# Two-stage routed attention and experts on one core: the second pair's preparation moved by two blocks, the output stage's rests on VectorE, value products copied by ScalarE, projections interleaved

## The chip, the cores and the metric

The kernel runs on one core of one Trainium2 chip. A core has TensorE (matrix products into PSUM), VectorE, ScalarE and GpSimd (elementwise work), and SyncE, which issues most of the transfers. Each engine works through its own list of instructions in the order in which they stand there; engines wait for each other through semaphores. The time is device microseconds of one execution, median of the runs shown; lower is better.

## What is computed

Three layers, one behind the other: attention with a cluster mask, a mixture of experts, and a gated convolution with an output projection.

```python
# attention, B=2, H=8, S=768, D=64
mask = q_assign[:, :, :, None] == k_assign[:, :, None, :]      # argmax over 16 centroids
attn = softmax(where(mask, q @ k.T / 8, -1e9));  out = attn @ v
# experts: every token goes to one of E=8, d_model 512, hidden 1024
h = np.maximum(x[b, s] @ w1[e], 0.0);  out[b, s] = p[e] * (h @ w2[e])
# last layer, per batch b: 768 tokens, 512 channels, 5 taps
gate = 1 / (1 + exp(-sum_k conv_w[k] * xp[:, k:k + S, :]))
return (gate * (x @ w_val)) @ w_out
```

## The kernel before

The program is written in one order by hand; every engine gets its instructions in that order, and each pool of buffers makes a writer wait until the buffer's last readers are done.

**Attention.** Eight pairs of heads, twelve blocks (`i`) to a pair; a block is one head and 128 queries against 768 keys. Block `i` issues the scores of block `i + 2` (`do_S`, L601: two products at L607 from the stacked tile `st`, two at L611 that also need its rows 64 to 79), transposes its own weights (`do_T`, L642), takes the exponential of block `i + 2` (`do_exp`) and at odd blocks a part of the product with V (L654). The next pair is prepared in six groups of steps (`prep_steps`, L322 and on), one group to a block, at `i % 12` = 0 to 5 (L769): keys rounded and centroid products (`k_hi`, `dots1`); queries (`q_hi`, `k_lo`, `dots2`); `argmax1` and `argmax2`; `q_lo` and six transfers `stack1` into `st`; `argmax3` and `argmax4`; `rows`, `rows_out` and four transfers `stack2`, which bring rows 64 to 79. Scores of the next pair are first wanted at `i % 12` = 10. Input tiles of keys and queries have one buffer, so the second pair's loads wait for the first pair's steps. All these transfers stand in SyncE's queue. The first pair's preparation stands in one list ahead of the loop, with five products without a use (`spin1`) between the first scores and the one-hot transposes (L438).

**Between attention and experts.** Tokens are scattered to expert slots by GpSimd's queue and read back by SyncE's (L897). TensorE meanwhile does 34 products without a use (`spin3`, bfloat16, 512 columns).

**Experts.** From L912 on TensorE transposes tokens and runs three products of rounded parts for every product (`hi` x `hi`, `hi` x rest, rest x `hi`), all in a 4-byte rounded type (fp32r) with 256 or 512 columns.

**Output stage** (L1054 to the end). Tokens are transposed (L1092), ScalarE rounds them (`xh`, L1096), a copy `xf` is kept, and GpSimd forms the rests `xl` = `xf` - `xh` (L1101). There are eight (batch, 128 channels) blocks. For each: the convolution is one ScalarE product and four VectorE multiply-adds (L1114), ScalarE takes the sigmoid (L1119), TensorE forms the value product in PSUM (L1128 to L1134, 24 products of 384 columns), VectorE multiplies both (L1147, which reads PSUM and so frees it), ScalarE rounds (`gh`, L1148) and GpSimd forms the rest `gl` (L1149). The projection of 128 tokens is twelve products of 512 columns (L1160 to L1163), copied out by ScalarE (L1164) and stored. In batch 1, `x2_tiles(1, ...)` stands ahead of the sigmoid, and six of the twelve projections stand behind the last block.

Of the kernel before, what the change touches and what calls it, by code (L numbers as in the profile page):

```python
# [18 lines left out]
S = 768  # L19
# [13 lines left out]
def routed_attention_moe_kernel(  # L33
# [45 lines left out]
    def load_kq(g, between=()):  # L79
# [3 lines left out]
        for dst, src in between:  # L83
            nc.sync.dma_start(dst, src)
        nc.sync.dma_start(X[g][:, 1, :], kq[b, p, :, 1, :])
# [8 lines left out]
    load_kq(0, [(cent_sb, cent), (cd, cdiag)])  # L94
# [11 lines left out]
    keep_warm(ps_m.tile([128, 512], F32, tag="m", name="spin0"), 9)  # L106

# [214 lines left out]
    def prep_steps(g):  # L322
# [413 lines left out]
    for grp in prep_steps(0):  # L736
        for f in grp:
            f()
    load_v(0)
    load_kq(1)  # L740
# [7 lines left out]
    for i in range(NI):  # L748
# [20 lines left out]
        if i % 12 < len(prep):  # L769
            for f in prep[i % 12]:  # L770
# [45 lines left out]
    keep_warm(ps_t.tile([128, 512], F32, tag="t", name="spin3"), 34)  # L816
# [261 lines left out]
    def x2_tiles(b, t0, n, eng):  # L1078
# [14 lines left out]
        for i in range(n):  # L1093
# [14 lines left out]
    def conv0(b, d):  # L1108
        G[b, d] = fl.tile([128, S], F32, tag="gt", name="gt", bufs=4)
# [11 lines left out]
    V = {}  # L1121
# [18 lines left out]

    def gated(b, d):
# [3 lines left out]
        gt, vp = G.pop((b, d)), V.pop((b, d))  # L1145
        gv = gt.rearrange("p (a c) -> p a c", a=2)
# [4 lines left out]
    def project(b, t, parts=1):  # L1151
        ts = slice(128 * t, 128 * t + 128)
        r0 = S * b + 128 * t
        os_ = fl.tile([128, 512], F32, tag="os", name="os")
        w = 512 // parts
        for n in range(parts):
            cs_ = slice(w * n, w * n + w)
            op = ps_x.tile([128, 512], F32, tag="x", name="op")
            for k in range(4):
                nc.tensor.matmul(op[:, :w], gh[b][:, k, ts], oh_[:, k, cs_], start=(k == 0), stop=False)  # L1160
                nc.tensor.matmul(op[:, :w], gh[b][:, k, ts], ol[:, k, cs_], start=False, stop=False)  # L1161
            for k in range(4):
                nc.tensor.matmul(op[:, :w], gl[b][:, k, ts], oh_[:, k, cs_], start=False, stop=(k == 3))  # L1163
            nc.scalar.copy(os_[:, cs_], op[:, :w])  # L1164
# [81 lines left out]
```

## Time and profile before

| | us |
|---|---|
| median of 3 runs | 584.48 (584.1 to 588.53) |
| the profiled execution, whole | 586.31 |
| its span, first to last instruction | 584.6 |
| TensorE busy | 553.5 (95%) |
| VectorE busy | 394.2 (67%) |
| ScalarE busy | 333.1 (57%) |
| GpSimd busy | 146.1 (25%) |

Attention takes the span's first 270 us, the experts stand from 282 to 484, the output stage from 489 to the end. A busy TensorE is not TensorE at its full clock: the page gives the granted clock apart. What one engine waits for is read from the timeline of a stretch, where each row has start, length, engine, line, operation, and in brackets the idle time ahead and what ended it.

### The profile page before, as it was taken

What the parts mean: (1) busy time and instruction counts of PE and PEld (TensorE: products, weight loads), DVE (VectorE), ACT (ScalarE), POOL (GpSimd) and SP (SyncE); (2) the same over time, 40 slices, a digit from 0 to 9 for tenths busy, and PEclk for the clock granted to TensorE, in tenths of its full rate; (3) what the DMA queues carried; (4) which work ended last, traced back from release to release, by engine and by line L of the source; (5) the groups of instructions that cost most, each with busy time, mean ns of one, the idle gap of its engine ahead of it and who ended that gap; (6) DMA issues with size and microseconds to landing.
All of it is one profiled execution on the core that took longest, in us unless ns stands there. A gap on an engine that the chain in (4) does not pass through costs nothing. (4 is left out here: it accounts for less than half of the span.)

```text
span 584.6 us, 9359 instructions
## 1 busy us (share of the span) xinstructions
PE 553.5 (95%) x3474; PEld 440.0 (75%) x3474; DVE 394.2 (67%) x644; ACT 333.1 (57%) x603; POOL 146.1 (25%) x121
## 2 busy tenths in 40 slices
PE   7799999999999999997899999999999996987997
PEld 3476767676767777774698988989989983885876
DVE  6376667676787876557378868769688361699940
ACT  3386868686868686852256545555564452453522
POOL 4100101010121210304431350531513351565220
PEclk8689999999999999998999999999999999898999
DMA  6958686764565646012567777778678585500112
GB/s 145 267 111 263 136 266 133 234 127 132 124 188 108 204 92 183 1 73 103 217 224 287 262 244 266 251 252 301 231 270 304 227 322 183 221 0 1 55 73 90
DMA packets 33103, 104.82 MB, mean 179 GB/s; under 512 B 5713, under 2 KB 6225, under 8 KB 27936
## 3 DMA queue, kind: packets, MB, share of 16 engines
q1 hardware_dynamic: 29104, 97.84, 53.8%
q0 software_dynamic: 3280, 6.32, 2.9%
q8 instruction: 28, 0.46, 0.3%
q10 hardware_dynamic: 672, 0.06, 0.1%
q14 instruction: 19, 0.16, 0.1%
HBM read 63.45 MB, written 24.95 MB: 151 GB/s over the span
## 5 line engine op out<-in xcount | busy, mean ns | idle before, releaser
L618 DVE TENSOR_REDUCE mx<-s 128x1 f32<-128x768 f32 x96 | 91.6, 955 | 59.6 <-PE s L611 53.8
L319 DVE TENSOR_TENSOR wlo<-wraw,whi 128x1024 fp32r<-128x1024 f32 x66 | 90.9, 1379 | 22.1 <-ACT whi L318 21.6
L647 ACT COPY pt<-tp 128x384 f32<-128x384 f32 x148 | 65.5, 481 | 57.7 <-PE tp L642 57.5
L627 ACT ACTIVATE pexp<-s,mx 128x768 f32<-128x768 f32 x96 | 87.0, 906 | 8.0 <-DVE mx L618 7.0
L318 ACT CAST whi<-wraw 128x1024 fp32r<-128x1024 f32 x68 | 70.0, 1043 | 29.9 <-DMA wraw<-in_wq_dram 29.7
L642 PE MATMUL tp<-ident,pexp 128*128 128x128 f32 x576 | 81.5, 278 | 0.4 <-ACT pt L647 0.3
L642 PEld LDWEIGHTS tp<-ident,pexp 128*128 128x128 f32 x576 | 68.6, 142 | 7.7 <-ACT pt L647 3.3
L654 PE MATMUL pv<-pt,vt 128*64 128x384 f32 x360 | 67.8, 498 | 0.1
L607 PE MATMUL s<-st 128*128 128x384 f32 x188 | 58.2, 391 | 1.8 <-ACT pexp L627 1.8
L977 PE MATMUL yp<-whi,hhi 128*128 128x512 f32 x136 | 53.8, 395 | 0.0
L981 PE MATMUL yp<-whi,hlo 128*128 128x512 f32 x136 | 53.7, 395 | 0.0
L980 PE MATMUL yp<-wlo,hhi 128*128 128x512 f32 x136 | 53.7, 395 | 0.0
L1114 DVE SCALAR_TENSOR_TENSOR gt<-xf,convw_sb,gt 128x768 f32<-128x768 f32 x32 | 51.5, 1626 | 1.7 <-ACT gt L1110 1.1
L611 PE MATMUL s<-st 80*128 80x384 f32 x188 | 49.7, 346 | 0.0
L954 ACT ACTIVATE hhi<-hps 128x512 fp32r<-128x512 f32 (+1 forms) x36 | 20.7, 575 | 50.0 <-PE hps L950 47.6
L337 POOL TENSOR_TENSOR xx<-xkq,xx 128x768 fp32r<-128x768 f32 x8 | 14.5, 1815 | 118.8 <-ACT xx L331 79.5
L236 POOL TENSOR_TENSOR wspace<-wspace 128x512 f32<-128x512 f32 x8 | 14.2, 1778 | 119.3 <-ACT wspace L232 108.7
L607 PEld LDWEIGHTS s<-st 128*128 128x128 f32 x188 | 29.0, 194 | 19.4 <-issue 8.6
L955 DVE SCALAR_TENSOR_TENSOR hlo<-hps,hhi 128x512 fp32r<-128x512 f32 (+1 forms) x36 | 23.6, 655 | 28.0 <-ACT hhi L954 28.0
L950 PE MATMUL hps<-xhi,whi 128*128 128x256 f32 x256 | 41.5, 283 | 0.7 <-ACT xhi L924 0.7
L950 PE MATMUL hps<-xlo,whi 128*128 128x256 f32 x256 | 40.7, 280 | 0.1
L950 PE MATMUL hps<-xhi,wlo 128*128 128x256 f32 x256 | 40.5, 279 | 0.0
(218 smaller groups left out, 978.1 us busy)
## 6 DMA issues: line engine op xcount, KB each, us to landing
wraw<-in_wq_dram SPq DMA_DIRECT2D x34, 1024.0 KB, 4.9
st<-xx SPq DMA_DIRECT2D x48, 384.0 KB, 5.5
xkq<-in_kq_dram SPq DMA_DIRECT2D x16, 384.0 KB, 4.5
xslots<-padrow SPq DMA_DIRECT2D x8, 514.0 KB, 8.0
wspace<-in_wd_dram SPq DMA_DIRECT2D x8, 512.0 KB, 5.7
xs<-xslots SPq DMA_DIRECT2D x7, 514.0 KB, 6.6
vt<-in_v_dram SPq DMA_DIRECT2D x8, 384.0 KB, 3.3
out_dram<-os SPq DMA_DIRECT2D x11, 256.0 KB, 2.0
```

The lines of the kernel that those rows point to most:

```text
L318: nc.scalar.copy(hi[:, c], t[:, c])
L319: (lo_eng or nc.vector).tensor_tensor(lo[:, c], t[:, c], hi[:, c].bitcast(F32), op=ALU.subtract)
L607: nc.tensor.matmul(ps[:, n, :384], st[:, 1, q0:q0 + 128], st[:, 0, 384 * n:384 * n + 384], start=True, stop=False)
L618: nc.vector.tensor_reduce(mx, ps[:, :, :384], axis=AX.XY, op=ALU.max, negate=True)
L627: nc.scalar.activation(pt, ps[:, :, :384], AF.Exp, bias=mx[:, 0:1], accum_out=Zt[i // 6][:, t, h:h + 1])
L642: nc.tensor.transpose(tp[:, k, :], p[:, 128 * kt:128 * kt + 128], ident)
L647: nc.scalar.copy(dst, tp)
L654: nc.tensor.matmul(PVs[u][64 * h:64 * h + 64, :], Vt[g][:, kt, h, :], PT[u, h][:, kt, :], start=(kt == 0), stop=(kt == NQT - 1), skip_grou ...
L950: nc.tensor.matmul(hp[:, fi, :w], a[:, d, fs], c[:, d, :w], start=(n + d == 0), stop=(n + d == 5))
L977: nc.tensor.matmul(yp[t], hhi[:, fa, ts], whv[:, f, :], start=(q == 0 and f == 0), stop=False)
L980: nc.tensor.matmul(yp[t], hhi[:, fa, ts], wlv[:, f, :], start=False, stop=False)
L981: nc.tensor.matmul(yp[t], hlo[:, fa, ts], whv[:, f, :], start=False, stop=(q == 1 and f == 3))
```

## The change

Six things are altered.

1. At the start the centroids are loaded ahead of the keys, and the first queries by ScalarE's queue; `cent_norm` stands ahead of `k_hi`; `spin1` has two products and not five; the second pair's keys and queries are loaded ahead of the first V.
2. The second pair's six groups of preparation stand at blocks 2 to 7 and not 0 to 5. The other pairs keep their places.
3. `spin3` has ten products and not 34, and is followed by 50 products of an fp32r tile of ones: 32 with 128, 192, 224 and 256 columns, 18 with 128, 192 and 288.
4. In the output stage the rests `xl` and `gl` are formed by VectorE; GpSimd has none of them.
5. ScalarE copies each value product to SBUF (`value_out`, three buffers), and VectorE multiplies from there. Tiles `gt` have three buffers and not four.
6. TensorE's order: value products run ahead by up to a block, projections of batch 0 begin at block 5, and those of batch 1 do three of four channel blocks for five token tiles ahead of the last. Some projections take their PSUM from the value products' pool. The last tile is copied in two halves by two engines and stored by two queues.

```diff
-    load_kq(0, [(cent_sb, cent), (cd, cdiag)])
+    nc.sync.dma_start(cent_sb, cent)
+    load_kq(0, nc.scalar)
+    nc.sync.dma_start(cd, cdiag)
...
-                k_hi, k_lo, cent_norm, q_hi, dots1, dots2, q_lo,
+                cent_norm, k_hi, k_lo, q_hi, dots1, dots2, q_lo,
...
-                lambda: keep_warm(ps_v.tile([128, 512], F32, tag="pv", name="spin1"), 5),
+                lambda: keep_warm(ps_v.tile([128, 512], F32, tag="pv", name="spin1"), 2),
...
+    load_kq(1)
     load_v(0)
-    load_kq(1)
     load_v(1)
...
-        if i % 12 < len(prep):
-            for f in prep[i % 12]:
+        ps = i % 12 - (0 if g else 2)
+        if 0 <= ps < len(prep):
+            for f in prep[ps]:
                 f()
...
-    keep_warm(ps_t.tile([128, 512], F32, tag="t", name="spin3"), 34)
+    keep_warm(ps_t.tile([128, 512], F32, tag="t", name="spin3"), 10)
+    spin4 = ps_t.tile([128, 512], F32, tag="t", name="spin4")
+    for w in (128, 192, 224, 256):
+        for _ in range(8):
+            nc.tensor.matmul(spin4[:, :w], onesr[:, :128], onesr[:, :w], start=True, stop=True)
+    for w in (128, 192, 288):
+        for _ in range(6):
+            nc.tensor.matmul(spin4[:, :w], onesr[:, :128], onesr[:, w:2 * w] if w < 256 else onesr[:, :w], start=True, stop=True)
...
-                    nc.gpsimd.tensor_tensor(
+                    nc.vector.tensor_tensor(
                         xl[b][:, d:d + 2, c0:c0 + 384], xf[b][:, d:d + 2, 4 + c0:388 + c0],
...
+    def value_out(b, d):
+        VS[b, d] = fl.tile([128, S], F32, tag="vs", name="vs", bufs=3)
+        nc.scalar.copy(VS[b, d].rearrange("p (a c) -> p a c", a=2), V.pop((b, d))[:, :, :384])
+
...
-        nc.vector.tensor_tensor(gv, gv, vp[:, :, :384], op=ALU.mult)
+        nc.vector.tensor_tensor(gt, gt, VS.pop((b, d)), op=ALU.mult)
         nc.scalar.copy(gh[b][:, d, :], gt)
-        nc.gpsimd.tensor_tensor(gl[b][:, d, :], gt, gh[b][:, d, :].bitcast(F32), op=ALU.subtract)
...
     after = {
-        1: [lambda: x2_tiles(1, 0, 2, nc.scalar.copy)],
-        2: [lambda: x2_tiles(1, 2, 2, nc.scalar.copy)],
-        3: [lambda: x2_tiles(1, 4, 2, nc.scalar.copy)],
-        6: [lambda: project(0, 0), lambda: project(0, 1)],
-        7: [lambda: project(0, 2), lambda: project(0, 3)],
+        1: [lambda: value(0, 2)],
+        2: [lambda: value(0, 3)],
+        3: [lambda: value(1, 0), lambda: value(1, 1)],
+        4: [lambda: value(1, 2)],
+        5: [lambda: value(1, 3), lambda: project(0, 0)],
+        6: [lambda: project(0, 1), lambda: project(0, 2)],
+        7: [lambda: project(0, 3), lambda: project(0, 4)],
     }
+    evict = {1: (0, 1), 2: (2,), 3: (3,), 4: (4, 5), 5: (6,), 6: (7,)}
...
     for n in range(1, 8):
         conv_a(*order[n], (1, 2))
-        for f in after.get(n, ()):
-            f()
         conv_b(*order[n - 1])
+        for m in evict.get(n, ()):
+            value_out(*order[m])
+        if n < 4:
+            x2_tiles(1, 2 * n - 2, 2, nc.scalar.copy)
         if n < 7:
             conv0(*order[n + 1])
         gated(*order[n - 1])
-        conv_a(*order[n], (3, 4))
-        if n > 1:
-            value(*order[n])
+        conv_a(*order[n], (3,))
+        gated_rest(*order[n - 1])
+        conv_a(*order[n], (4,))
+        for f in after[n]:
+            f()
...
-    for t in range(6):
-        project(1, t, 2 if t == 5 else 1)
+    for t in range(5):
+        project_terms(1, t, range(3))
+    for t in range(5):
+        project_terms(1, t, (3,))
+        project_out(1, t)
+    project_terms(1, 5, range(4))
+    project_out(1, 5, 2)
```

TensorE's list at the loop's first blocks, before; `s` are scores, `tp` a block's transposes, `dott` the second pair's centroid products, `dots` their transposes.

```order
L607 MATMUL s<-st_192 128x384 x2
L611 MATMUL s<-st_192 128x384 x2
L642 MATMUL tp<-ident,pexp 128x128 x6
L349 MATMUL dott<-xkq,cd 32x384 x4
L607 MATMUL s<-st_193 128x384 x2
L611 MATMUL s<-st_193 128x384 x2
L642 MATMUL tp<-ident,pexp 128x128 x6
L359 MATMUL dots<-ident,dsb 128x128 x3
```

The same place in the changed kernel, from its third block on.

```order
L609 MATMUL s<-st_194 128x384 x2
L613 MATMUL s<-st_194 128x384 x2
L644 MATMUL tp<-ident,pexp 128x128 x6
L351 MATMUL dott<-xkq,cd 32x384 x4
L609 MATMUL s<-st_195 128x384 x2
L613 MATMUL s<-st_195 128x384 x2
L644 MATMUL tp<-ident,pexp 128x128 x6
L361 MATMUL dots<-ident,dsb 128x128 x3
```

The rows are alike, but two blocks (scores and transposes) now stand ahead of the first `dott`.

TensorE's list between attention and experts, in the changed kernel: the new products stand behind the ten that are left of `spin3` and ahead of the first expert's transposes.

```order
L823 MATMUL spin_3248<-onesr 128x128 x8
L823 MATMUL spin_3248<-onesr 128x192 x8
L823 MATMUL spin_3248<-onesr 128x224 x8
L823 MATMUL spin_3248<-onesr 128x256 x8
L826 MATMUL spin_3248<-onesr 128x128 x6
L826 MATMUL spin_3248<-onesr 128x192 x6
L826 MATMUL spin_3248<-onesr 128x288 x6
L922 MATMUL xp<-ident,xs 128x128 x8
```

Before, 24 more rows of `spin3` stood in their place.

VectorE's list in the output stage, before, from the first conv on.

```order
L1114 SCALAR_TENSOR_TENSOR gt<-xf,convw_sb,gt 128x768 x6
L1147 TENSOR_TENSOR gt<-gt,vp 128x768
L1114 SCALAR_TENSOR_TENSOR gt<-xf,convw_sb,gt 128x768 x4
L1147 TENSOR_TENSOR gt<-gt,vp 128x768
L1114 SCALAR_TENSOR_TENSOR gt<-xf,convw_sb,gt 128x768 x4
```

The same place in the changed kernel.

```order
L1124 SCALAR_TENSOR_TENSOR gt<-xf,convw_sb,gt 128x768 x6
L1160 TENSOR_TENSOR gt<-gt,vs 128x768
L1124 SCALAR_TENSOR_TENSOR gt<-xf,convw_sb,gt 128x768
L1165 TENSOR_TENSOR gl<-gt,gh 128x768
L1124 SCALAR_TENSOR_TENSOR gt<-xf,convw_sb,gt 128x768 x3
L1111 TENSOR_TENSOR xl<-xf,xh 128x2x384 x2
L1160 TENSOR_TENSOR gt<-gt,vs 128x768
L1124 SCALAR_TENSOR_TENSOR gt<-xf,convw_sb,gt 128x768
L1165 TENSOR_TENSOR gl<-gt,gh 128x768
```

The rests have come in between, and the multiply reads the copy `vs` in SBUF and not PSUM.

## Rows read from the trace of the kernel before

**Rows 1.** The page's first line.
```profile
span 584.6 us, 9359 instructions
```

**Rows 2.** Timeline of the start: start us, us, engine, line, operation, [idle before].
```profile
12.38 0.56 DVE L382 TENSOR_TENSOR oh<-wts,arr 128x384 bf16<-128x384 f32 x1
12.94 2.32 PE L104 MATMUL spin<-onesb 128*128 128x512 bf16 x5
15.19 1.71 PE L438 MATMUL pr<-identb,oh 128*16 128x128 bf16 x24
19.82 1.01 PE L607 MATMUL s<-st 128*128 128x384 f32 x2 [1.34 <-ACT pexp L627]
```

**Rows 3.** Timeline of the first pair's blocks, with the second pair's preparation among them.
```profile
24.02 1.49 PE L349 MATMUL dott<-xkq,cd 128*32 128x384 f32 x2 [1.28 <-DMA xkq<-in_kq_dram]
26.59 1.50 PE L349 MATMUL dott<-xkq,cd 128*32 128x384 f32 x6 [1.08 <-DMA xkq<-in_kq_dram]
31.24 0.99 PE L607 MATMUL s<-st 128*128 128x384 f32 x2
35.76 1.12 DVE L340 SCALAR_TENSOR_TENSOR xx<-xkq,xx 128x768 fp32r<-128x768 f32 x1
36.98 0.61 PE L607 MATMUL s<-st 128*128 128x384 f32 x2 [0.29 <-ACT pexp L627]
48.78 0.61 PE L607 MATMUL s<-st 128*128 128x384 f32 x2
```

**Rows 4.** Stretch 24 to 28 us: busy time by engine, granted clock, DMA share, GB/s.
```profile
24.00:28.00 4.00, 2.90 (x8) 0.38 (x8) 0.00 (x0) 0.99 (x3) 1.80 (x1) 0.50 0.92 333
```

**Rows 5.** SyncE's queue for the second pair; last row: L411's time to landing, issued 45.46.
```profile
36.90 0.61 SPq L405 DMA_DIRECT2D st<-xx  x1
45.46 1.66 SPq L411 DMA_DIRECT2D st<-ohr  x1
DMA to landing us min/median/max: 3.7/3.7/3.7
```

**Rows 6.** Timeline between attention and experts; last row: line L945, durations in ns.
```profile
271.60 9.19 PE L104 MATMUL spin<-onesb 128*128 128x512 bf16 x34
274.96 5.33 PEld L104 LDWEIGHTS <-onesb 128*128 128x128 bf16 x25 [0.28 <-issue]
282.38 1.21 PE L912 MATMUL xp<-ident,xs 128*128 128x128 f32 x8 [1.60 <-DMA xs<-xslots]
286.47 0.63 PE L950 MATMUL hps<-xhi,whi 128*128 128x256 f32 x4
286.94 0.63 PE L950 MATMUL hps<-xhi,wlo 128*128 128x256 f32 x4
L945 PE MATMUL hps<-xfull,wfull x64: 270/275/275, 460.3 to 467.3; 128*128 128x128 f32 x64
```

**Rows 7.** Timeline of the output stage, VectorE and GpSimd.
```profile
502.10 8.29 DVE L1114 SCALAR_TENSOR_TENSOR gt<-xf,convw_sb,gt 128x768 f32<-128x768 f32 x6 [1.07 <-ACT gt L1110]
537.93 5.67 DVE L1114 SCALAR_TENSOR_TENSOR gt<-xf,convw_sb,gt 128x768 f32<-128x768 f32 x4
538.96 1.84 POOL L1149 TENSOR_TENSOR gl<-gt,gh 128x768 fp32r<-128x768 f32 x1 [4.61 <-ACT gh L1148]
```

**Rows 8.** Groups by line, 488 to 586 us: busy us, mean ns | idle before.
```profile
L1096 ACT CAST xh<-x2p 128x512 fp32r<-128x512 f32 x12 | 7.0, 589 | 12.3 <-PE x2p L1092 12.3
L1119 ACT ACTIVATE gt<-gt 128x768 f32<-128x768 f32 x8 | 6.8, 851 | 11.8 <-DVE gt L1114 11.8
```

**Rows 9.** Chain that ended last, two pieces; then a stretch as in rows 4.
```profile
566.44 0.92 PE op L1163 x4
581.40 0.37 ACT os L1164
532.00:536.00 4.00, 4.00 (x18) 4.00 (x18) 3.96 (x3) 1.24 (x3) 1.83 (x1) 0.69 0.00 0
```

**Rows 10.** Line L1165, the stores of the result: issue to landing.
```profile
DMA to landing us min/median/max: 1.7/2.0/2.2
```

More of the change, by code (lines that the diff above doesn't have):

```diff
@@ L77, in routed_attention_moe_kernel, with load_kq @@
     X, Vt, ST = {}, {}, {}
-    def load_kq(g, between=()):
+    def load_kq(g, q_queue=None):
         b, p = pairs[g]
@@ L82, in load_kq @@
         nc.sync.dma_start(X[g][:, 0, :], kq[b, p, :, 0, :])
-        for dst, src in between:
-            nc.sync.dma_start(dst, src)
-        nc.sync.dma_start(X[g][:, 1, :], kq[b, p, :, 1, :])
+        (q_queue or nc.sync).dma_start(X[g][:, 1, :], kq[b, p, :, 1, :])
     def load_v(g):
@@ L106, in routed_attention_moe_kernel @@
     keep_warm(ps_m.tile([128, 512], F32, tag="m", name="spin0"), 9)
+    onesr = cst.tile([128, 384], F32R, name="onesr")
+    nc.scalar.copy(onesr, onesb[:, 0:1].to_broadcast([128, 384]))
     ident = cst.tile([128, 128], F32, name="ident")
@@ L1108, in conv0 @@
     def conv0(b, d):
-        G[b, d] = fl.tile([128, S], F32, tag="gt", name="gt", bufs=4)
+        G[b, d] = fl.tile([128, S], F32, tag="gt", name="gt", bufs=3)
         nc.scalar.activation(G[b, d], xf[b][:, d, 0:S], AF.Copy, scale=convw_sb[:, d, 0:1])
@@ L1119, in conv_b @@
         nc.scalar.activation(G[b, d], G[b, d], AF.Sigmoid)
-    V = {}
+    V, VS, GT = {}, {}, {}
     def value_hi(b, d, c):
@@ L1144, in gated, with gated_rest, project_terms, project_out @@
             gl[b] = fx.tile([128, 4, S], F32R, tag="xl", name="gl")
-        gt, vp = G.pop((b, d)), V.pop((b, d))
-        gv = gt.rearrange("p (a c) -> p a c", a=2)
-        nc.vector.tensor_tensor(gv, gv, vp[:, :, :384], op=ALU.mult)
+        gt = G.pop((b, d))
+        nc.vector.tensor_tensor(gt, gt, VS.pop((b, d)), op=ALU.mult)
         nc.scalar.copy(gh[b][:, d, :], gt)
-        nc.gpsimd.tensor_tensor(gl[b][:, d, :], gt, gh[b][:, d, :].bitcast(F32), op=ALU.subtract)
-    def project(b, t, parts=1):
-        ts = slice(128 * t, 128 * t + 128)
+        GT[b, d] = gt
+    def gated_rest(b, d):
+        nc.vector.tensor_tensor(
+            gl[b][:, d, :], GT.pop((b, d)), gh[b][:, d, :].bitcast(F32), op=ALU.subtract
+        )
+    OP = {}
+    def project_terms(b, t, ks):
+        ts = slice(128 * t, 128 * t + 128)
+        if (b, t) not in OP:
+            if (6 * b + t) % 5 < 2:
+                OP[b, t] = ps_x.tile([128, 512], F32, tag="x", name="op")
+            else:
+                OP[b, t] = ps_g.tile([128, 2, 512], F32, tag="v", name="op")[:, 0, :]
+        op = OP[b, t]
+        for k in ks:
+            nc.tensor.matmul(op, gh[b][:, k, ts], oh_[:, k, :], start=(k == 0), stop=False)
+            nc.tensor.matmul(op, gh[b][:, k, ts], ol[:, k, :], start=False, stop=False)
+            nc.tensor.matmul(op, gl[b][:, k, ts], oh_[:, k, :], start=False, stop=(k == 3))
+    def project_out(b, t, parts=1):
+        op = OP.pop((b, t))
         r0 = S * b + 128 * t
@@ L1157, in project @@
             cs_ = slice(w * n, w * n + w)
[L1158 to L1164, printed above, removed]
-            nc.sync.dma_start(out[r0:r0 + 128, cs_], os_[:, cs_])
+            (nc.vector.tensor_copy if n else nc.scalar.copy)(os_[:, cs_], op[:, cs_])
+            (nc.scalar if n else nc.sync).dma_start(out[r0:r0 + 128, cs_], os_[:, cs_])
+    def project(b, t):
+        project_terms(b, t, range(4))
+        project_out(b, t)
     for t in range(6):
@@ L1191, in routed_attention_moe_kernel @@
         gated(*order[n - 1])
-        conv_a(*order[n], (3, 4))
-        if n > 1:
-            value(*order[n])
+        conv_a(*order[n], (3,))
[3 more added lines that the diff above has]
+            f()
     conv_b(1, 3)
     gated(1, 3)
-    for t in (4, 5):
-        project(0, t)
-    for t in range(6):
-        project(1, t, 2 if t == 5 else 1)
+    gated_rest(1, 3)
+    project(0, 5)
+    for t in range(5):
[5 more added lines that the diff above has]
+    project_out(1, 5, 2)
     fin.close()
```

## The prediction

> **What bounds the kernel now.** I read the granted clocks and the page first, then the timeline in the three places the change touches, then the chain of work that ended last. The span is 584.6 us [rows 1]; the profiled execution took 586.31 us, 1.8 us over the median of 584.48. I take differences on the span and subtract them from the median. TensorE is busy nearly everywhere, so time can be won only where it waits or runs at the lower of its clocks, and a wait put into its list is paid in full unless it falls into a gap that is there already. Three such places matter.
>
> *The first blocks.* TensorE starts the loop's scores at 19.82 us [rows 2]. In the first block it stands at the second pair's centroid products, which wait 1.28 and 1.08 us for keys and queries and take 1.5 us each; they end at 28.1, and the next block's scores come behind them [rows 3]. Between 24 and 28 us the granted clock is 0.50, the 1.2 GHz level [rows 4].
>
> *Between attention and experts.* The spins run from 271.60 to 280.79, and the first expert's transposes wait until 282.38 for their tokens [rows 6]: a gap of 1.6 us, behind which TensorE never rests until the experts end.
>
> *The output stage.* Four conv steps of VectorE take 5.67 us, and in their middle stands one rest of GpSimd with 1.84 us [rows 7]. Without it they would take (5.67 - 1.84) / 4 = 0.95 us each. So VectorE stands still for as long as GpSimd works, and TensorE waits for VectorE, since only the multiply frees PSUM.
>
> **The change, part by part.**
>
> *Start.* The one-hot rows are ready at 12.38 + 0.56 = 12.94, but their transposes start at 15.19, behind five spins of 2.32 us [rows 2]. Three fewer save 3 x 0.46 = 1.4 us; the most there is to win is 15.19 - 12.94 = 2.25. The load order changes little in my view: the same bytes are on the way, keys come later and queries a little earlier. I take -1.6 us, so that scores start at 18.2; the bounds are 0 (transposes at the lower clock eat the gain) and -2.25. For the second queue the Trainium skill has a rule (Trainium Kernel Development and Optimization, Key Constraints): queues of several engines share the same 16 DMA engines, and a second one saves issue time alone. That speaks against a gain from loading the queries by ScalarE's queue; no row here shows two such loads at once.
>
> *Second pair moved.* Blocks 0 and 1 no longer stand behind the load. But the preparation itself is two blocks later. When does it end? Blocks 0 and 1 at the low clock cost at most what block 1 costs now, 31.24 - 28.1 = 3.15; I take 3.0 each. Blocks 2 and 3 now carry the steps of keys and queries; between the 1.91 of a block at full clock ((36.98 - 31.24) / 3) and 3.15 I take 2.5 each, nearer the former, since TensorE no longer rests and its clock should rise. From the block with the argmax steps to the end of `q_lo` it is now 35.76 + 1.12 - 31.24 = 5.64 us [rows 3]. Sum from the first scores: 6.0 + 5.0 + 5.6 = 16.6, so `q_lo` ends at 34.8 and not 36.88.
>
> What is late next is the transfers behind `q_lo`. SyncE's queue issues five `stack1` transfers and then `stack2`, one behind the other; the last of the first head lands at 45.46 + 3.7 = 49.16, 12.3 us behind the end of `q_lo` [rows 5]. The next pair's scores start at 48.78 [rows 3], and their second half, which needs these rows, half a us later: they just meet. After the move that landing is at 34.8 + 12.3 = 47.1, while block 5 starts at 18.2 + 12.9 = 31.1 and would want it 12.3 us later (49.3 - 36.98), at 43.4. So the second pair's scores wait about 3.7 us on TensorE, and what stands behind them (transposes, products with V, the next scores) waits too, with ScalarE and VectorE behind that. The gain is 49.16 - 47.1 = 2.1 us and not the 5.9 us that the blocks have won. A rest of that length may drop the clock, as at 532 to 536, where it is 0.69 behind a rest [rows 9]: (1 - 0.69) / 0.5 x 4 = 2.5 us at half speed, so 1.2 us lost at most. I take 0.3 of it, -1.8 in all; bounds -0.5 and -5.9.
>
> *Spins.* The tenth old spin starts at 274.96 [rows 6], so the new ones start near 275.3. No row shows an fp32r product under 256 columns. From below: one column per cycle and no less than what a weight load allows; the 256-column products stand 0.47 / 4 = 0.118 us apart [rows 6]. Then 50 products cost 50 x 0.12 = 6.0 us, end at 281.3, inside the gap, and cost nothing: the gap's tokens cover them. From above: as plain float32, where a 128-column product is two passes of (467.3 - 460.3) / 63 = 0.111 us [rows 6], 0.22 us, and in proportion to columns: 8 x (0.22 + 0.33 + 0.39 + 0.12) + 6 x (0.22 + 0.33 + 0.13) = 12.6 us. They end at 287.9, which is 5.5 us behind the 282.38 at which the tokens are there, and the experts start that much later. I take nothing, by the row of the same type with 256 columns, of which 224 is the near neighbour; both ends stay in the range. The Trainium skill (TensorE: Matmul & The Clock Gate, LDWEIGHTS) gives a weight load as columns over 1.2 GHz, 0.107 us for 128; by it the 50 would cost about 5.4 us, also inside the gap. The trace's 0.111 and 0.118 agree.
>
> *Output stage.* VectorE takes 16 rests from GpSimd (8 `xl`, 8 `gl`), each near the 0.95 us of a conv step of the same shape, 15.2 us in all; it loses the standing still. ScalarE takes eight value copies, near the 0.85 us of a sigmoid of that shape [rows 8]. Walking the queues: conv starts at 502.1 as now, since the first four `xl` fall where VectorE waits for tokens. Up to the end of the third block's conv VectorE has 12 conv steps, two multiplies, two `gl`, two `xl`: 18 x 0.95 = 17.1 us. It waits 4.1 us: the first multiply 0.9 for its value copy; the first `gl` 2.4, because its rounding stands on ScalarE behind the sigmoid, two value copies, four copies of tokens and a first conv product; the first `xl` of batch 1 0.8. So 523.3. Then ScalarE does sigmoid, value copy and three token copies, 3.1 us [rows 8]: at 526.4 the last tokens of batch 1 are rounded. TensorE has by then done four and a third value blocks and rested about 5 us. From there it has no more rest: 88 value products at 0.23 x 3/4 = 0.173, 15.2 us; 144 projection products at 0.92 / 4 = 0.23, 33.1 us [rows 9]; and the same 1.2 us for a low clock behind that rest. End: 575.9. The last five copies now come 0.7 us apart, but have two buffers, which are free only when stored, 2.0 us later [rows 10]: 0.6 us. With 0.3 from the last product to its copy and 0.37 for that, it ends near 577.2 against 581.77 [rows 9]: -4.6 us. Bounds: without VectorE's 4.1 us of waits -8.7; with as much again -0.5.
>
> Sum: -1.8 + 0 - 4.6 = -6.4, so 584.5 - 6.4 = 578.1 us. (The start's -1.6 is inside the -1.8.)
>
> **The rivals.**
>
> *Narrow products cost plain passes.* +5.5 us before the experts: 583.6. For it: nothing shows that the rounded type keeps its rate there. Against it: the neighbour at 256.
>
> *The stack transfers don't bind.* If the second pair's rows land within 8.6 us of `q_lo` and not 12.3, the first blocks keep 5.9: 584.5 - 5.9 - 4.6 = 574.0. For it: the queue has less on the way at that time. Against it: the transfers go one behind the other, and the two scores now meet the landing to within 0.2 us.
>
> *Slower.* The new spins don't hold the clock up, and cost plain passes at the half clock: 25.2 us from 275.3, to 300.5, 18 us behind the tokens: 584.5 + 18.1 - 6.4 = 596.2. It decides from 282.38 - 275.3 + 6.4 = 13.5 us of new spins on. For it: nothing but that the type is unseen; against it: fp32r products elsewhere run at the full clock.
>
> **How the numbers follow.** Forecast 0.50, its own range 575.5 to 581; plain passes 0.32, 580.5 to 586; no binding of transfers 0.14, 571.5 to 576.5; slower 0.04. About 1% (5.8 us, so 578.7 and 590.3) is what a measurement of this kernel can tell from no change. Faster by over 1%: 0.6 of the forecast, nearly all of the third case, 0.02 of the plain passes: 0.46. Slower by over 1%: the last case: 0.04. Within 1%: 0.50. The range 573.0 to 584.5 leaves out a part of the third case (0.04), the upper third of the plain passes (0.10) and the last case.
>
> **What would show it.** In the changed trace: the second pair's first scores (L613) idle 3 to 4 us for a DMA near 43 to 47, and stand at about 47; the spins' last row ends before the transposes L922, whose idle is for `xs`; VectorE's conv steps all near 0.95 us with GpSimd empty from 489 on; TensorE with one rest near 521 to 526 and none from there on. The forecast is wrong if the 50 products take over 7 us, if L613 finds its rows landed, or if TensorE rests again behind 526 because ScalarE, which now has value copies and projections in one list, is late.

## The result and the profile after

The changed kernel takes 581.62 us (median of 20 runs, 577.94 to 585.87), the kernel before, run beside it, 588.2 (20 runs, 582.9 to 592.28). The ratio is 0.9904, 95% interval [0.9876, 0.9933]: 5.6 us less, between 3.9 and 7.3 (the two medians lie 6.6 apart). The median of three runs from which the prediction subtracted, 584.48, was 3.7 us under that of twenty.

```profile
span 580.1 us, 9383 instructions
PE 9%; DVE 3%; ACT 3%; DMA 1%; issue 0%; ACTq 0%
L613 PE MATMUL s<-st 80*128 80x384 f32 x188 | 49.1, 342 | 2.4 <-DMA st<-ohr 2.4
L960 PE MATMUL hps<-xhi,whi 128*128 128x256 f32 x256 | 41.9, 284 | 1.6 <-issue 0.9
```

These four lines are from the page of the changed kernel: its span, the chain that ended last by engine, and two groups (operation, shapes, count, busy us and mean ns of one, idle us before and its releaser). TensorE leads the chain now (before: VectorE 6%, TensorE 5%). All idle time ahead of `L613` is one wait of 2.4 us for the second pair's rows. The last line has 1.6 us of rest among the experts' first products, "issue" for the most part: TensorE waited for nothing that the profile shows. That was not forecast.

The timeline of the changed kernel (start us, us, engine, line, operation, idle before) in the first blocks, with VectorE's `q_lo` and SyncE's transfer among them; of before [rows 2, 3, 5]:

```profile
6.62 1.50 PE L351 MATMUL dott<-xkq,cd 128*32 128x384 f32 x8 [1.47 <-DMA cd<-in_cd_dram]
...
9.74 3.10 PE L422 MATMUL s<-xx 64*128 64x384 f32 x12
...
13.74 2.73 PE L440 MATMUL pr<-identb,oh 128*16 128x128 bf16 x24
...
19.12 0.61 PE L609 MATMUL s<-st 128*128 128x384 f32 x2 [1.15 <-ACT pexp L629]
...
31.43 1.11 DVE L342 SCALAR_TENSOR_TENSOR xx<-xkq,xx 128x768 fp32r<-128x768 f32 x1
...
41.19 1.63 SPq L413 DMA_DIRECT2D st<-ohr  x1
...
44.55 0.59 PE L613 MATMUL s<-st 80*128 80x384 f32 x2 [2.44 <-DMA st<-ohr]
```

The scores start at 19.12 and not 19.82. `q_lo` ends at 32.54 and not 36.88; the second half of the second pair's scores stands at 44.55, 12.0 us behind it.

Between attention and experts and in the experts' first 20 us [rows 6]:

```profile
267.03 4.43 PE L104 MATMUL spin<-onesb 128*128 128x512 bf16 x10
270.90 4.74 PE L823 MATMUL spin<-onesr 128*128 128x128 f32 x32
275.47 2.30 PE L826 MATMUL spin<-onesr 128*128 128x128 f32 x18
...
278.69 0.63 PE L922 MATMUL xp<-ident,xs 128*128 128x128 f32 x4 [0.92 <-DMA xs<-xslots]
...
280.88 0.99 PE L960 MATMUL hps<-xhi,whi 128*128 128x256 f32 x4 [0.72 <-ACT xhi L934]
...
287.28 1.04 PE L922 MATMUL xp<-ident,xs 128*128 128x128 f32 x8
...
294.66 0.49 PE L960 MATMUL hps<-xhi,whi 128*128 128x256 f32 x2 [0.43 <-issue]
...
296.11 0.36 PE L960 MATMUL hps<-xlo,whi 128*128 128x256 f32 x1 [0.45 <-issue]
...
297.54 0.72 PE L960 MATMUL hps<-xhi,whi 128*128 128x256 f32 x4 [0.45 <-issue]
...
301.86 1.03 PE L922 MATMUL xp<-ident,xs 128*128 128x128 f32 x8
```

The experts' first product comes 3.43 us earlier (280.88 for 284.31). From 294.66 on TensorE advances in bursts 1.45 us apart. The transposes of the second and the third expert's tokens (L922) stand 14.58 us apart, where before they stood 12.19 apart. In the kernel before, the first product and these two transposes are:

```profile
284.31 0.99 PE L950 MATMUL hps<-xhi,whi 128*128 128x256 f32 x4 [0.72 <-ACT xhi L924]
...
290.71 1.04 PE L912 MATMUL xp<-ident,xs 128*128 128x128 f32 x8
...
302.90 1.04 PE L912 MATMUL xp<-ident,xs 128*128 128x128 f32 x8
```

The output stage, VectorE and TensorE [rows 7, 9]:

```profile
500.17 1.83 DVE L1111 TENSOR_TENSOR xl<-xf,xh 128x768 fp32r<-128x768 f32 x2
501.91 6.16 DVE L1124 SCALAR_TENSOR_TENSOR gt<-xf,convw_sb,gt 128x768 f32<-128x768 f32 x6
...
511.90 0.96 DVE L1165 TENSOR_TENSOR gl<-gt,gh 128x768 fp32r<-128x768 f32 x1 [2.03 <-ACT gh L1161]
...
519.10 0.34 PE L1139 MATMUL vp<-xh,wlo 128*128 128x384 f32 x1
...
524.93 0.69 PE L1138 MATMUL vp<-xh,whi 128*128 128x384 f32 x1 [5.49 <-ACT xh L1106]
...
575.30 0.40 PE L1182 MATMUL op<-whi,gl 128*128 128x512 f32 x1
...
576.76 0.42 DVE L1191 COPY os<-op 128x256 f32<-128x256 f32 x1 [16.40 <-ACT os L1191]
```

Six conv steps take 6.16 us where they took 8.29. TensorE rests once, 5.5 us for the last token tiles, and from 524.93 to 575.30 no more.

### The profile page after: what moved, and what is told of

Same layout as the page of the kernel before. It is cut to its first block, busy times and chain, and to the rows that moved or that the text cites. A ratio compares the mean times of both kernels' runs of the same rounds, so it can differ in the third digit from the quotient of the medians.

```text
span 580.1 us, 9383 instructions
## 1 busy us (share of the span) xinstructions
PE 550.8 (95%) x3485; PEld 442.6 (76%) x3485; DVE 386.5 (67%) x661; ACT 338.7 (58%) x611; POOL 114.6 (20%) x105
## 5 line engine op out<-in xcount | busy, mean ns | idle before, releaser
L613 PE MATMUL s<-st 80*128 80x384 f32 x188 | 49.1, 342 | 2.4 <-DMA st<-ohr 2.4
L656 PEld LDWEIGHTS pv<-pt,vt 128*64 128x64 f32 x360 | 21.9, 136 | 24.1 <-issue 23.7
```

Source lines behind the costliest of these rows:

```text
L656: nc.tensor.matmul(PVs[u][64 * h:64 * h + 64, :], Vt[g][:, kt, h, :], PT[u, h][:, kt, :], start=(kt == 0), stop=(kt == NQT - 1), skip_grou ...
```

## Why one pair of profiles was not enough

The table puts the executions that follow beside the two first ones (two more, in which the experts themselves are altered, come at the end). Each number is read from the kernel's timeline: start of the first loop scores, end of the second pair's `q_lo`, first spin behind attention, the experts' first product, the experts from there to the start of the last scaled copy of their results, from that start to the first conv step, and from there to the end of the span.

| us | scores | q_lo end | first spin | experts start | experts last | copy to conv | conv to end |
|---|---|---|---|---|---|---|---|
| before | 19.82 | 36.88 | 271.60 | 284.31 | 200.2 | 17.6 | 82.5 |
| spin_alone | 17.20 | 36.65 | 271.26 | 283.50 | 204.9 | 16.3 | 82.1 |
| out_alone | 17.20 | 36.61 | 271.25 | 284.11 | 205.8 | 18.4 | 79.2 |
| load_alone | 16.77 | 34.10 | 268.88 | 281.82 | 203.0 | 16.5 | 82.9 |
| pair_alone | 17.95 | 32.69 | 268.39 | 280.29 | 205.2 | 16.6 | 82.8 |
| offset0 | 18.03 | 33.25 | 267.87 | 280.36 | 204.4 | 18.0 | 78.5 |
| offset1 | 17.97 | 32.29 | 266.61 | 279.29 | 204.2 | 17.8 | 78.6 |
| after | 19.12 | 32.54 | 267.03 | 280.88 | 202.8 | 18.2 | 78.2 |
| after_again | 19.05 | 32.88 | 267.38 | 280.55 | 203.7 | 18.4 | 79.3 |
| rests_gpsimd | 18.95 | 32.37 | 266.83 | 280.39 | 203.0 | 16.8 | 82.4 |
| tokens_early | 19.18 | 32.65 | 267.11 | 280.58 | 203.0 | 18.8 | 73.9 |
| combo | 18.02 | 31.52 | 265.94 | 279.66 | 204.4 | 17.8 | 72.2 |

Among kernels with the same code there, the end of `q_lo` and the start of the experts repeat to within 0.9 us, and so does the first spin but for pair_alone. The scores and the experts do not, and there the profile on which the prediction stood was an unusual one. Its experts took 200.2 us, while eleven other executions, whose experts have the same instructions in the same order, took 202.8 to 205.8. And its scores started at 19.82, while three others with the old start had them at 16.8 to 17.2.

## Experiments: which part carries what

Each result below is the ratio to the kernel before, run beside it, with its 95% interval in brackets. First the changed kernel once more.

> The changed kernel once more. In its first profile the experts (first expert product to the last scaled copy of their results) took 202.8 us (280.88 to 483.68) where the kernel before took 200.2 (284.31 to 484.50); 2.4 us of that went between 287 and 298 us, where ScalarE started its Relu copies up to 4.7 us late. Theory 'chance': that stall is an event of that one execution, the experts take 200.2 here and the span is near 577.5. Theory 'coupled': the experts give back what an earlier start brings, they take 202.8 again, at the same place, and the span is near 580. Ratio to the kernel before 0.988 by the first, 0.992 by the second.

Ratio 0.9888 [0.9846, 0.9931], experts 203.7: the experts' time fits "coupled", the ratio "chance". The next runs show that the longer experts do not come from the change.

Then single parts, each put into the kernel before: pair_alone has the start and the second pair (parts 1 and 2), spin_alone the spins (part 3), out_alone the output stage (parts 4 to 6). Of each its main lines:

```diff
-                lambda: keep_warm(ps_v.tile([128, 512], F32, tag="pv", name="spin1"), 5),
+                lambda: keep_warm(ps_v.tile([128, 512], F32, tag="pv", name="spin1"), 2),
...
-        if i % 12 < len(prep):
+        ps = i % 12 - (0 if g else 2)
```

```diff
-    keep_warm(ps_t.tile([128, 512], F32, tag="t", name="spin3"), 34)
+    keep_warm(ps_t.tile([128, 512], F32, tag="t", name="spin3"), 10)
+    spin4 = ps_t.tile([128, 512], F32, tag="t", name="spin4")
...
```

```diff
-                    nc.gpsimd.tensor_tensor(
+                    nc.vector.tensor_tensor(
...
+    def value_out(b, d):
...
```

> The kernel before with only the start and the second pair's preparation changed. Theory 'the pair carries the first half': first spin product behind attention at 267.0 us (271.6 in the kernel before), second half of the waited-for scores at 44.5, and the output stage as before (81.8 us from the first read-back wait, 2.4 us per convolution step where GpSimd shares its time); whole time -4.6 us, ratio 0.992. Rival 'it is given back in the experts': -2.2 us, ratio 0.996, with the experts at 202.6 us. Rival 'the gain at the transition needs the narrow products': the span does not follow the 4.6 us and the expert stage starts less than 3 us earlier, because 34 spin products of 0.22 us now end later than the tokens.

> The kernel before with only the 34 wide spin products replaced by 10 wide and 50 narrow fp32r ones. Theory 'covered': the last spin ends about 2 us before the tokens' transposes, these and the first expert product start as before (282.4 and 284.3), whole time 0, ratio 1.000. Rival 'four passes': the narrow products take 0.25 us each, end 5 us behind the tokens, +5 us, ratio 1.009. Rival 'the spins bring on the stall in the experts': the experts take 202.8 us instead of 200.2, +2.4 us, ratio 1.004.

> The kernel before with only the output stage changed. Theory 'the output stage is worth what it shows in the changed kernel': from the last expert copy to the end of the span 96.4 us instead of 100.1, -3.7 us, ratio 0.994, one rest of TensorE of 5 to 6 us for the last token tiles and none behind it. Rival 'with the original start it is worth the 4.6 us that were forecast': ratio 0.992. Rival 'part of it is the experts' shift': under -2 us, ratio above 0.997.

pair_alone: 0.9923 [0.9888, 0.9957]; spin_alone: 1.0016 [0.9982, 1.0051]; out_alone: 0.9967 [0.993, 1.0005]. The pair carries more than half (-4.5 us), the spins nothing (+0.9, not clear of zero), the output stage less than was forecast (-1.9, by itself not clear of zero). Together they make -5.5, near the -5.6 of the whole change. In pair_alone the granted clock fell to 0.61 in the stretch 44 to 48 us, behind the wait for the rows, and its first spin is 1.3 us later than in the other kernels with the same blocks: the drop that the prediction priced at 1.2 us. The same stretch is granted 1.00 in the changed kernel (first row pair_alone, second the changed kernel; columns as in [rows 4]):

```profile
44.00:48.00 4.00, 3.30 (x13) 3.14 (x14) 1.42 (x2) 1.18 (x3) 0.00 (x0) 0.61 0.71 172
44.00:48.00 4.00, 3.29 (x22) 2.59 (x24) 2.78 (x4) 1.83 (x5) 0.00 (x0) 1.00 0.74 190
```

The drop came in one of six executions with a wait of 2.4 to 2.6 us, and its cost does not show at the experts' start, which is 280.29 in pair_alone and 280.35 to 280.88 in the other five. The experts lost time in all three, in spin_alone and out_alone without an earlier start: the stall belongs to the kernel before too.

What the old start does when undisturbed shows in out_alone, in its timeline and in the stretch 9 to 13 us (columns as in [rows 4]):

```profile
9.61 1.77 PE L420 MATMUL s<-xx 64*128 64x384 f32 x12
...
12.77 1.51 PE L438 MATMUL pr<-identb,oh 128*16 128x128 bf16 x24 [0.20 <-DVE oh L382]
...
17.20 0.62 PE L607 MATMUL s<-st 128*128 128x384 f32 x2 [1.34 <-ACT pexp L627]
```

```profile
9.00:13.00 4.00, 3.64 (x25) 2.40 (x26) 3.57 (x7) 0.00 (x0) 0.00 (x0) 1.00 0.83 168
```

The granted clock is 1.00, the 2.4 GHz level; twelve products take 1.77 us, and the transposes `pr` start 0.20 behind the one-hot rows, with all five spins ahead of them. In the first profile of before the same stretch was granted 0.50, the 1.2 GHz level, and the same products took 3.10:

```profile
9.91 3.10 PE L420 MATMUL s<-xx 64*128 64x384 f32 x12
```

```profile
9.00:13.00 4.00, 3.89 (x16) 3.16 (x17) 3.61 (x6) 0.00 (x0) 0.00 (x0) 0.50 0.83 170
```

There the spins took 2.32 us and were the late ones [rows 2]. The new start takes 3.1 us for these twelve in all ten executions that have it. The centroids' second tile `cd` now lands late, and TensorE rests 1.3 to 2.0 us for it ahead of its first products (1.47 at 6.62 above). That this rest is what makes the twelve slow is not shown, and the granted clock does not settle it: the stretch is granted 0.50 in four of the ten and 1.00 in six, among these the changed kernel's first profile, where the twelve took 3.10 all the same:

```profile
9.00:13.00 4.00, 4.00 (x16) 3.14 (x17) 3.45 (x6) 0.06 (x1) 0.26 (x2) 1.00 0.88 180
```

Next, where the second pair's preparation stands, and its load alone. offset1 is the changed kernel with the first line below (offset0 has a 0 there), load_alone the kernel before with the second piece.

```diff
-        ps = i % 12 - (0 if g else 2)
+        ps = i % 12 - (0 if g else 1)
```

```diff
+    load_kq(1)
     load_v(0)
-    load_kq(1)
```

> The changed kernel with the second pair's preparation one block later than the first block instead of two. In the changed kernel TensorE waits 2.4 to 2.6 us at 42.1 us for the second pair's rows, which land 12.0 us behind the end of q_lo (32.5). Theory 'transfers bind, and the load is early enough': q_lo ends one block (1.7 to 2.4 us) earlier, the wait shrinks to 0 to 0.8 us, the first spin behind attention starts at 265.2 instead of 267.0 to 267.4; ratio to the kernel before 0.986. Rival 'the blocks are only fast because the preparation is kept out of them': the centroid products wait over 1 us for keys or queries in the second block and the clock is slow there, the first spin starts at 267.5 or later, ratio 0.990 or more.

> The changed kernel with the second pair's preparation where it was before the change, in the first blocks; its load still goes out ahead of the two value loads. Theory 'the earlier load does it, not the move': centroid products wait less than 1 us for keys and queries, q_lo ends near 29, TensorE does not wait for the rows, the first spin starts at 264.7 to 265.5, ratio 0.985. Rival 'the move does it': they wait 1 us and more as before, at the lower clock, q_lo ends near 34 to 36, the first spin starts at 268 to 271, ratio 0.992 to 0.997.

> The kernel before with one line moved: the second pair's keys and queries are loaded ahead of the first pair's values instead of behind them; preparation, start, spins and output as before. First spin behind attention so far: 271.6, 271.3, 271.2 in kernels with the old order; 267.1 (mean of four) with the whole start and pair change, 267.9 with it and the preparation not moved. Theory 'the earlier load carries most of it': the centroid products no longer wait 1.28 and 1.08 us, second half of the waited-for scores 2 us earlier than 49.3, first spin at 269.0 to 269.6, ratio 0.996. Rival 'the start carries it, and the load changes nothing by itself': first spin at 271 or later, ratio 1.000.

offset1: 0.9903 [0.987, 0.9935]; offset0: 0.9888 [0.9826, 0.995]; load_alone: 0.9957 [0.9924, 0.999].

```profile
22.64 1.49 PE L349 MATMUL dott<-xkq,cd 128*32 128x384 f32 x2 [4.16 <-DMA xkq<-in_kq_dram]
...
25.18 1.50 PE L349 MATMUL dott<-xkq,cd 128*32 128x384 f32 x6 [1.04 <-DMA xkq<-in_kq_dram]
...
32.99 1.11 DVE L340 SCALAR_TENSOR_TENSOR xx<-xkq,xx 128x768 fp32r<-128x768 f32 x1
...
46.45 0.53 PE L611 MATMUL s<-st 80*128 80x384 f32 x2
```

In load_alone (timeline) the waits for keys and queries did not go, 4.16 and 1.04 us, since its scores start earlier; but the products behind them stand 1.4 us earlier than in [rows 3] (1.0 earlier than in spin_alone and out_alone, whose scores start as early and which wait 4.86 and 4.50 us for the keys), `q_lo` ends 2.8 earlier, and the first spin 2.5 earlier than in the three kernels with the old load order (268.88 for a mean of 271.37). Theory and rival of that run both missed in part: the load carries most, though not by the waits that it was to remove. In offset0, which has the new start as well, the first spin is 1.0 earlier still (267.87), although its scores start 1.3 later: TensorE waits once for the load, 1.76 us. Moving the blocks by two adds 0.8 more (a mean of 267.1 over five), by one 1.3 (266.61) to 2.5 (265.35, in combo_overflow_late below). offset0 fell between its two theories, with a wait for the load but none for the rows; so did offset1, where the wait for the rows shrank to 1.30 us and one of 1.58 for the queries stayed. The ratios of the three positions cannot be told apart. By the first spin one block comes first in all three executions that have it (265.35 to 266.61, for 266.83 to 268.39 with two); offset0 is a single execution inside the spread of two blocks.

The transfer chain held everywhere: in all nine executions where TensorE waits for the rows it gets them 12.0 us behind the end of `q_lo`. In offset0 and load_alone, which show no wait, the scores come 12.4 us behind `q_lo`; if the rows take 12.0 there too, they have just landed.

For the output stage, rests_gpsimd is the changed kernel with the rests back on GpSimd (the same edit for `gl`), tokens_early the changed kernel with ScalarE's copies of the second batch's last four token tiles earlier:

```diff
-                    nc.vector.tensor_tensor(
+                    nc.gpsimd.tensor_tensor(
```

```diff
-        1: [lambda: value(0, 2)],
-        2: [lambda: value(0, 3)],
+        1: [lambda: value(0, 2), lambda: x2_tiles(1, 2, 2, nc.scalar.copy)],
+        2: [lambda: [value_hi(0, 3, c) for c in range(2)], lambda: x2_tiles(1, 4, 2, nc.scalar.copy),
+            lambda: [value_lo(0, 3, c) for c in range(2)]],
```

> The changed kernel with the sixteen rests of the output stage back on GpSimd, all else as changed (value copies by ScalarE, interleaved projections). Theory 'a rest on GpSimd stops VectorE': six convolution steps take 8.3 to 9.3 us instead of 6.2, two gl and two xl more at 1.84 instead of 0.95 before the last tokens are rounded; from the first convolution step to the end 82 to 84 us instead of 78.2 to 79.4, while that step itself starts 1.8 us earlier; ratio to the kernel before 0.993 to 0.999. Rival 'the gain of the output stage is the value copies and the order of TensorE': 78 to 80 us, ratio 0.986 to 0.990.

> The changed kernel with ScalarE's copies of the second batch's last four token tiles one block earlier each. Theory 'TensorE sets the end of the output stage from the moment the last tokens are rounded': its rest of 5.5 us at 519.4 and the lower clock behind it go, the last copies come 6 to 7 us earlier; from the first convolution step to the end of the span 72.5 us instead of 78.2 to 79.4; ratio to the kernel before 0.979. Rival 'VectorE sets the end': ScalarE's copies push its sigmoids and value copies back, VectorE's last multiply comes later than 55.6 us behind the first convolution step, TensorE rests before the last products, and the gain is under 2 us, ratio 0.987 to 0.990.

rests_gpsimd: 0.996 [0.9932, 0.9987]; tokens_early: 0.9832 [0.9761, 0.9902]. With the rests back on GpSimd (timeline, VectorE, TensorE and GpSimd):

```profile
500.20 8.99 DVE L1124 SCALAR_TENSOR_TENSOR gt<-xf,convw_sb,gt 128x768 f32<-128x768 f32 x6 [1.07 <-ACT gt L1120]
...
526.39 0.69 PE L1138 MATMUL vp<-xh,whi 128*128 128x384 f32 x1 [7.80 <-ACT xh L1106]
...
496.30 7.98 POOL L1111 TENSOR_TENSOR xl<-xf,xh 128x768 fp32r<-128x768 f32 x4 [8.13 <-DVE xf L1107]
```

Six conv steps take 8.99 us again, TensorE rests 7.8, and from the first conv step to the end it is 82.4, as in the four kernels with the old output stage (82.1 to 82.9). So value copies and the new order of TensorE give nothing behind the first conv step without the rests' move. Whether that move alone would give the whole gain, without them, no run shows. The Trainium skill (SBUF — State Buffer, section on SBUF's two separate sides) states an exclusive lock of VectorE and GpSimd on a shared port pair, for which the loser stands still; the trace agrees, with 2.8 us more for six steps beside GpSimd. But the same run also has the conv 1.4 us earlier behind the last expert copy (16.8 for 17.8 to 18.8): this is what VectorE's first four `xl` cost, the last two of them with 1.83 us at 500.17, right ahead of the conv.

In tokens_early (timeline of TensorE, and VectorE's last row):

```profile
521.20 0.44 PE L1138 MATMUL vp<-xh,whi 128*128 128x384 f32 x1 [2.15 <-ACT xh L1106]
...
573.00 0.42 DVE L1191 COPY os<-op 128x256 f32<-128x256 f32 x1 [16.44 <-ACT os L1191]
```

The rest is 2.15 us and not 5.49, and the last copy starts 70.6 us behind the first conv step (502.36) and not 74.9. TensorE does set the end from the moment the last tokens are rounded. The run had expected 72.5 from conv to end and 0.979; it got 73.9 and 0.9832, with 2.15 us of the rest still there.

## Experiments: the stall among the experts

In the first 15 us of the experts GpSimd issues twelve indirect writes of overflow rows. overflow_late is the changed kernel with them held back until `do_mm1(1)` is done:

```diff
+            nc.gpsimd.tensor_copy(warm[:, 0:1], HT[1][0][:, 7, 0:1].bitcast(F32))
+            for tt in range(12):
+                scatter(xover, idx1[:, tt:tt + 1], xnat[:, tt, :], NCH * 128, "rows of different tokens")
```

combo is tokens_early with offset 1 and the last four token copies ahead of ScalarE's second `gh`; combo_overflow_late is combo with the writes late and the 64-bit weight chunks begun at the third expert:

```diff
+        if n == 2:
+            late = []
+            for c in range(2):
+                value_hi(0, 3, c)
+            x2_tiles(1, 4, 2, nc.scalar.copy, late)
         gated(*order[n - 1])
```

```diff
-    XS["ready"] = True
...
+        if k == 2:
+            XS["ready"], XS["catch"] = True, 8
```

> The changed kernel with GpSimd's twelve indirect writes of overflow rows held back until the second expert's first products are done (by a one-element copy ahead of them that reads that result), some 25 us later. The experts took 200.2 us in the kernel before's first profile, and 202.8, 203.7, 205.2, 204.9 and 205.8 in five others, three of these with the same instructions there; what they lose lies in the first 15 us, where TensorE advances in bursts 1.45 us apart and ScalarE starts copies up to 6.2 us late, while these writes are under way. Theory 'the indirect writes do it': no such bursts in the first 15 us, experts at 200.2 us or less, ratio 0.981 to 0.984 (unless the same comes back 25 us later). Rival 'something else does it': bursts at the same place, experts 202 to 206 us, ratio 0.988 to 0.990.

> tokens_early with the second pair's preparation one block earlier, and ScalarE's last four token copies ahead of its rounding of the second gated block (the rests of these tokens behind VectorE's multiply and gl). In tokens_early TensorE still rests 2.15 us for the last token tile, and first convolution step to end is 73.9. Theory 'TensorE sets the end': that rest falls under 0.7 us, 72.4 us, first spin at 266.6, ratio to the kernel before 0.978 to 0.980. Rival 'VectorE sets the end by now': its last gl does not come earlier than 53.3 us behind the first convolution step and TensorE rests before the last products, 73.9 us or more, ratio 0.982 to 0.984.

> combo with the twelve indirect writes behind the second expert's first products again, and the loads of the 64-bit weight chunks, whose buffers these writes free and which stood ahead of the experts' weights in SyncE's queue, started one expert later. With the writes late alone, transposes of the second to the third expert's tokens were 12.19 us apart as in the first profile of the kernel before (14.6 to 16.4 in the others), but the weights behind such a load came 20 us late. Theory 'the writes cause the bursts only among the first loads': 12.2 us at the first place, no such bursts at 305 to 325, experts at 200.2 to 201, ratio 2.5 to 3 us below combo, 0.973 to 0.976. Rival 'they cause it wherever they stand': TensorE advances in bursts or waits at 305 to 325 and the experts take 202.5 to 206, ratio as combo.

overflow_late: 1.0208 [1.0146, 1.027]; combo: 0.978 [0.9746, 0.9814]; combo_overflow_late: 0.9817 [0.9785, 0.9849]. From overflow_late, the transposes of the second and third expert's tokens, SyncE's queue, and two stretches:

```profile
286.75 1.04 PE L922 MATMUL xp<-ident,xs 128*128 128x128 f32 x8
...
298.94 1.03 PE L922 MATMUL xp<-ident,xs 128*128 128x128 f32 x8
...
296.30 0.33 SPq L306 DMA_DIRECT2D wraw<-in_wq_dram  x1
...
323.88 0.33 SPq L229 DMA_DIRECT2D wspace<-in_wd_dram  x1
324.31 0.38 SPq L306 DMA_DIRECT2D wraw<-in_wq_dram  x1
```

```profile
300.00:310.00 10.00, 10.00 (x68) 9.12 (x68) 4.94 (x8) 4.72 (x7) 2.34 (x4) 1.00 0.05 19
310.00:320.00 10.00, 2.87 (x13) 1.96 (x11) 0.00 (x0) 0.00 (x0) 7.67 (x8) 0.84 0.03 0
```

Without the writes there, the two transposes stand 12.19 us apart, with no burst between. The loss that follows comes from the edit itself. The load of a weight chunk (L229) goes into the buffer that the writes read from; it stands in SyncE's list ahead of the experts' own weights (L306), waits for all twelve writes, and for 27 us nothing is issued: TensorE is busy 2.87 us of ten. In combo_overflow_late, where that load stands further back:

```profile
284.91 1.04 PE L924 MATMUL xp<-ident,xs 128*128 128x128 f32 x8
297.10 1.03 PE L924 MATMUL xp<-ident,xs 128*128 128x128 f32 x8
```

```profile
310.00:320.00 10.00, 10.00 (x66) 9.03 (x65) 3.64 (x4) 4.80 (x6) 7.74 (x7) 1.00 0.66 243
330.00:340.00 10.00, 5.91 (x20) 3.87 (x19) 9.44 (x16) 3.03 (x4) 2.44 (x2) 0.83 0.43 176
```

Again 12.19, and now TensorE is busy all of 310 to 320 while the writes are under way. It loses more at 330 to 340, where VectorE (9.44 of 10) has the weight chunks at twice the pace to catch up, and TensorE waits 2.79 and 1.30 us for its `wlo`; the experts take 207.7 us, and the kernel is no faster than combo (576.95 us for 575.21). So the bursts go with the writes standing among the experts' first loads: they are there in eleven executions with the writes in that place, where the two transposes stand 14.58 to 17.01 us apart, and not in the two with the writes elsewhere. The writes are not enough, though: the first profile of before has them in that place and no bursts. What slows TensorE there, which waits for nothing that the profile shows, stays open; and no version tried here turned it into time.

combo beats both kernels: 575.21 us (median of 6) beside 588.1. From its first conv step (501.84) the last copy (570.70) comes 68.9 us later. Of its theory, the time held, while TensorE rests 1.38 and 0.25 us, now for VectorE's `xl`.

## Why the prediction came out as it did

The sum was -6.4 us and the result is -5.6 (-3.9 to -7.3), but the terms behind it were off in both directions; 578.1 was forecast, and the ratio makes 578.9 of the 584.5 it was made against. In the order of its steps:

- **The start, -1.6.** Wrong. The step that failed is "Three fewer save 3 x 0.46 = 1.4 us", with "The load order changes little in my view". The five spins were late in one execution of four, the one in which the twelve products ahead of them took 3.10 us. Against the three other executions of the old start the new one's scores are 0.8 to 2.4 us later (17.95 to 19.18 for 16.8 to 17.2): `cd` now lands last, and the twelve products take 3.1 us each time. Only against the first profile of before are the scores earlier, by 0.7.
- **The second pair, -1.8 with the start.** The wait was right: TensorE waits for rows that land 12.0 us (forecast 12.3) behind `q_lo`. Mis-sized were the blocks ahead of it: from the first scores to the end of `q_lo` 13.4 us and not 16.6, so the wait is 2.4 and not 3.7 and the scores stand at 44.55 and not 47.1. By the first spin the term is -4.3 (267.1 for 271.4, means of five and three executions; -4.1 with pair_alone as a sixth), by the experts' first product -3.5 (six executions for three). Most of it, -2.5 by one execution of load_alone, is the load ahead of the values, which the working had put down to the moved blocks.
- **Spins, 0.** Right. The 50 narrow products take 6.5 us (spin_alone) to 6.9 and end ahead of the tokens.
- **Output stage, -4.6.** The walk through the queues came out right to 0.2 us: from the first conv step to the end of the last copy 75.1 forecast (577.2 - 502.1), 75.3 measured (577.2 - 501.9); one rest of 5.5 us for a forecast 5, VectorE's wait for the first `gl` 2.0 for 2.4, TensorE's last product at its end at 575.7 for 575.9. Two errors in it cancel, which is luck: the last tokens are rounded 23.0 us behind the first conv step and not 24.3, since VectorE waits 2.6 and not 4.1, and from there to the last product it is 50.8 and not 49.5. The step that failed is "conv starts at 502.1 as now, since the first four `xl` fall where VectorE waits for tokens". VectorE has no such room: the last two stand between the last token copy and the conv, the first two push the later copies back. Measured against several executions, conv to end is -3.8 (78.7 for 82.6), the way there +1.4, and the stage -2.4.
- **The experts, nothing.** The subtraction from one profile took 200.2 us for granted. In this stage the first comparison of profiles shows +2.6, since the first profile of before happened not to have the stall: 2.4 us of it lie between the two transposes, and 2.4 to 4.8 in the eleven executions with bursts.

So -3.5 and -2.4 make -5.9, near the measured -5.6, where -1.8 and -4.6 were forecast. Two terms were mis-sized in opposite directions, and that the sum came within 1 us is luck. The rivals fell. Plain passes would have shown 12.6 us of narrow products and not 6.9. That the transfers don't bind is refuted by the wait at L613. The slower case needed 13.5 us of new spins. One sum was off: the chance of faster by over 1% comes to 0.45 from its parts and not 0.46.

## What to carry to other kernels

A term read from one profile needs a second execution of the same code beside it: here the same instructions took 200.2 to 205.8 us in one stage and started 2.6 us apart in another. Moving work off an engine that blocks another pays only net of the place where it lands: the output stage won 3.8 us behind the first conv step and lost 1.4 ahead of it. A transfer that waits for a late buffer blocks everything behind it in its queue (27 us of SyncE's in overflow_late), so a reordering has to be followed through the issuing engine's list too.

## What the runs showed of the hardware

- fp32r products of 128, 192 and 288 columns cost on average about what those of 256 columns cost: 18 of them, each behind a weight load of its own, took 2.30 us. That is 0.128 each, or about 0.117 from start to start, beside 0.118 for 256 columns in [rows 6].
- A rest of TensorE of 2.4 us, the granted clock at 1.00 ahead of it, left the clock there in five of six executions (1.00 in 44 to 48 us in the changed kernel); in the sixth it fell to 0.61 in that stretch, and the first spin came 1.3 us later. Behind the rest of 5.5 us in the output stage the stretch 524 to 528 was granted 0.50.
- With GpSimd's indirect writes among the experts' first loads, TensorE's products came in bursts up to 1.45 us apart for some 4 us in eleven of twelve executions, with no releaser of TensorE in the profile, and ScalarE stood idle up to 6.24 us ahead of one of its copies (3.41 at most there in the first profile of before). Moved by 25 us, they left TensorE busy for 10.00 of 10 us (combo_overflow_late, 310 to 320).
